# Float32-to-bf16 copies on GpSimd instead of VectorE in a fused attention and SSM kernel, with the schedule replanned

## The chip, the cores and the metric

The kernel runs on one core of a Trainium2 chip. The metric is device time in microseconds for one launch. The core has TensorE (PE, matrix products; PEld is its weight load), VectorE (DVE), ScalarE (ACT), GpSimd (POOL) and SyncE (SP), which issues nearly all DMAs here. Each engine takes its instructions in the order in which the program gives them.

## The reference

What is computed from x (2048 rows of 512) is a mix of two branches, `g * a + (1 - g) * b`:

```python
g = sigmoid((x * gate_w).sum(-1, keepdims=True))
# a: attention, 32 heads of 16, all 2048 x 2048 scores, no mask
p = softmax(einsum("bhqd,bhkd->bhqk", q, k) * 16 ** -0.5)
a = einsum("bhqk,bhkd->bhqd", p, v) @ wo        # heads joined
# b: a long convolution of each of the 512 channels, in float32 by FFT
P = exp(dt * A * l)                             # 512 x 128 complex, l = 0..2047
K = einsum("dn,dnl,dn->dl", C, P, dt * B).real
b = conv(x, K)[:2048] + x * Dskip
```

## The kernel before, in words

**Attention.** For every block b (one head pair's rows of 512 queries; 32 blocks) there are 16 key quads (kt 0 to 15) of four score tiles of 128 x 512, 2048 tiles in all. Three tiles make a group; there are 683 groups, numbered g or x. `qk(g)` computes a group's scores into one of two PSUM buffers (SC), `ex(g)` has ACT take the exponentials (ET, EX), and `pvq` multiplies them into the block's sums (OA).

**Sets.** ACT does not take all exponentials. `decide` may start a set: three key quads, whose twelve tiles are laid out over four groups so that the third tile of each group goes to DVE. There `bits` turns it into 16-bit patterns that read as bf16 exponentials (DZ), and `batch` adds three constants to all four tiles of the set with 64-bit integer adds on POOL (DU); `sums` multiplies DZ and the three DU into OA, an average of four approximations. Whether a set may start is said by this line, where `win(x)` asks for four groups since the last start and for fewer sets than `due(x)`, which runs linearly between the points of PACE:

```python
if kt < DVK - 1 and win(x) is not None and idle() >= plan["used"] \
        and (kt < DVL or not sets or f"dvp{len(sets) - 1}" in sch.flag):
```

DVK and DVL are 14; the flag `dvp{i}` is set when set i's last product has been planned. ACT's instruction has two tiles in a group with a DVE tile, and three otherwise.

**The convolution kernel K.** From parameters on DVE (`params`, `params2`) powers of the decay are built by squaring and product. `digit` writes them out as bf16 pairs (DT), `powers` and `weights` build tables for each of four quarters qr of the channels (B16, Z), with `low` and `cast` turning float32 results into bf16. `zpart` extends Z, `tables` multiplies B16 with DT (T), and `kstage(blk)` has PE multiply T with Z, transposes the result on DVE (Kt) and copies it to Ks, from where SP stores it (kd) for the convolution.

**The convolution.** `yloads` loads x (U) and K (H, in a ring of buffers that grows at the load given in HS) and `ystage` multiplies them on PE; DVE applies the gate (Yst), SP stores and reloads it (Yl). `outs` and the tail multiply the attention result with wo and add both.

**The order of work.** A planner in the kernel (`Prog`, `Sched`) runs while the program is built. Each piece of work is a segment of a thread with an engine, a cost and a priority; for every group, `fill` places the segments whose planned time comes before ACT's. The planned order is the program's order on each engine. Ops marked `lk` (float32 or bf16 work on DVE whose inputs are all in SBUF, and POOL's adds) are kept apart in the plan: a POOL op that would meet such a DVE op gets a wait for it. FILL and LOW say how much work PE should have for each group (before and after group ZEND = 260); what lacks is filled with idle products of zeros (wm).

Of the kernel before, what the change touches and what calls it, by code (L numbers as in the profile page):

```python
# [39 lines left out]
FILL = 1500  # L40
LOW = 1300
SURP = 256
FILL2 = 1500
OVER = 0.5
REST = (14, 0, 1792, 425)
# [18 lines left out]
WIN = ((0, 560, 2, 4), (560, 679, 4, 6))  # L64
PACE = ((0, 0), (40, 0), (90, 0), (140, 0), (200, 15.0), (270, 28.3), (340, 39.5), (420, 53.9), (500, 73.9), (570, 90.7), (630, 105.7), (683, 118.95))
DVEND = 679
YLP = 4.5
YQ = 0
XGO = 'g14'
YGO = 'projs'  # L70
YLGO = 'K15'
BG0 = 'g0'
BG1 = 'g0'
BG2 = 'K4'
BG3 = 'g0'
TP = 2
KP = 0.4
NB = 2
# [5 lines left out]
US = [2, 12, 3]  # L84
HS = [4, 48, 8]
BACK = 0.4
# [16 lines left out]
SPILL = 3  # L103
DVCAP = 6
DVK = 14
JS = ((2, 0, 3, 1), (1, 0, 2, 3), (0, 2, 1, 3))
DVL = 14
VW = 136
VG = 4 * VW + 16
# [629 lines left out]
def record(nc, p, B, ins):  # L739
# [138 lines left out]
    todo = []  # L878
    plan = dict(q=0, at=0, used=0.0, prev=None, wait=None, x=0)

# [9 lines left out]
    def decide(g):  # L890
        while len(tiles) < min(3 * g + 3, NSL):
            q, x = plan["q"], len(tiles) // 3
            kt = q % 16
            if kt == 0:
                plan["wait"] = None
            plan["used"] = max(plan["used"], idle() - DVCAP)
            if kt < DVK - 1 and win(x) is not None and idle() >= plan["used"] \
                    and (kt < DVL or not sets or f"dvp{len(sets) - 1}" in sch.flag):
                w = win(x)
                plan["x"] = x  # L900
                c = q if kt else q + 1
                a, b = [y for y in range(q, q + 3) if y != c]
                own, late = [4 * a + k for k in range(4)] + [4 * b + k for k in range(4)], [4 * c + k for k in JS[len(tiles) % 3]]
                js = JS[len(tiles) % 3]
                k = 0
                for _ in range(12):
                    if len(tiles) % 3 == 2:
# [12 lines left out]
                for k, x in enumerate(us):  # L920
                    held_u[x] = (len(sets) - 1, k)
                qs, plan["q"] = [a, b], q + 3
            else:
                tiles.extend(range(4 * q, 4 * q + 4))
                qs, plan["q"] = [q], q + 1
            for y in qs:
                if y < NQ - 1:
                    todo.append((y, plan["prev"], plan["wait"]))
# [211 lines left out]
    def square(o, x, conj=False):  # L1140
# [8 lines left out]
        tt("DVE", half(o, 0), half(t1, 0), half(t1, 1), ALU.subtract, [(t1, 0)], [(o, 0)], F5)  # L1149

    def digit(n):

        m, x = DIGITS.index(n), B[n]
        for qr in range(4):
            d = B[f"DT{qr}"]
            yield ("DVE", .45)
            op("DVE", lambda v, d=d, qr=qr: v.tensor_copy(d(6 * P * m, [[2 * P, 2], [2, P], [1, 2]]), x(P * qr, [[D, 2], [1, P], [0, 2]])), [(x, 0)], [(d, (m, 0))], c=.07 + .28)
            op("DVE", lambda v, d=d, qr=qr: v.tensor_scalar(d(6 * P * m + 4 * P, [[2, P], [1, 2]]), x(D + P * qr, [[1, P], [0, 2]]), -1.0, None, ALU.mult), [(x, 0)], [(d, (m, 1))], c=.07 + .14)
        sch.mark("D" + n)
# [31 lines left out]
    def params2():  # L1191
# [20 lines left out]
        yield from digit("L64")  # L1212
        yield from cmul("L80", "L64", "L16")
# [3 lines left out]
        yield from short("M9", "")  # L1217
        yield from digit("L80")

# [3 lines left out]
    def ftk(i, h):  # L1223
        return [(FT[i], x) for x in HF[h]]
# [16 lines left out]
    def weights(qr):  # L1241
# [7 lines left out]
        def cast(part, l):  # L1249
            yield ("DVE", .3)  # L1250
            op("DVE", lambda v: v.tensor_copy(Z(part * l8 + 128 * l, [[1, 256]]), FP(part * e8 + 128 * l, [[1, 256]])), rw(l, l + 1), top, c=.21)

# [26 lines left out]

    def powers(qr, last, top):  # L1280

# [36 lines left out]
        def low(part, h):  # L1318
            yield ("DVE", .55)
            op("DVE", lambda v: v.tensor_copy(place(part, h, 4), FP(part * e8 + 128 * h, [[256, 4], [32, 4], [1, 32]])),  # L1320
               rw(*range(h, 8, 2)), [top[part]], c=.42)

# [11 lines left out]
        yield from cross(3, lambda part: FP(part * e8 + 768, one), rw(6), one)  # L1334
        yield ("DVE", .4)
        op("DVE", lambda v: v.memset(FP(0, one), 1.0), [], rw(0), c=.1)
        op("DVE", lambda v: v.memset(FP(e8, one), 0.0), [], rw(0), c=.1)
        op("DVE", lambda v: v.tensor_copy(last(256, [[l8, 2], [512, 4], [2, 32]]), fp(qr, ZT["L8"], [[PS, 2], [32, 4], [1, 32]])), fk(qr, ZT["L8"]), lo, c=.34)
# [14 lines left out]
    def zpart(qr):  # L1353
# [8 lines left out]
        def mul(u, i):  # L1362
            k, dn, at, part = units[u]
            Dm, xr, yr = B[dn], i, part if i == 0 else 1 - part
            yield ("DVE", H10)
            tt("DVE", lambda: FT[i].b16(1024 * (u % 2), [[128, 8], [1, 128]]), lambda: Z(xr * 4096, [[128, 8], [1, 128]]),
               lambda: Dm(yr * D + 128 * qr, [[0, 8], [1, 128]]), ALU.mult,
               [(Z, 3, qr), (Z, 5, qr), (Dm, (0, 0))] + ([(Dm, (0, 1))] if dn == "DL32" else []), ftk(i, u % 2), H10)

# [19 lines left out]
    def park():  # L1389
# [7 lines left out]
        sch.mark("pd")  # L1397

    def ploads():
        yield ("AFTER", "pd")  # L1400
        for qr, go in enumerate((BG0, BG1, BG2, BG3)):
            Z = B[f"Z{qr % NZ}"]
            yield ("AFTER", go)
            if qr >= NZ:
                yield ("AFTER", f"KT{4 * (qr - NZ) + 3}")
            for k0, n, over, at in ((0, 2, [3, 5], 256), (2, 2, [(1, 0), (1, 1)], 640), (4, 1, [(0, 0), (0, 1)], 1024), (5, 3, [(2, 0), (2, 1)], 1536)):
# [7 lines left out]
    def bases():  # L1414
        for qr, go in enumerate((BG0, BG1, BG2, BG3)):
            yield ("AFTER", go)
            B16 = B[f"B16{qr % NB}"]
            if qr >= NB:
                yield ("AFTER", f"T{4 * (qr - NB) + 3}")
            yield from powers(qr, B16, [(B16, 0), (B16, 2)])  # L1420
            yield from weights(qr)
# [4 lines left out]
    def tables():  # L1426
        for qr in range(4):
# [3 lines left out]
            for blk in range(4 * qr, 4 * qr + 4):  # L1431
                Tm, c0 = B[f"T{tbuf(blk)}"], CB * (blk % 4)
                bk = [(B16, 0), (B16, 2), (B16, (1, 0)), (B16, (1, 4))]
                old = [k for k in range(blk) if tbuf(k) == tbuf(blk)]
# [22 lines left out]
    def kstage(blk):  # L1457
        qr = blk // 4
        Z, Ks = B[f"Z{qr % NZ}"], B[f"Ks{blk % 2}"]
        zk = [(Z, 3, qr), (Z, 5, qr)] + [(Z, (k, p_), qr) for k in range(3) for p_ in range(2)]  # L1460
        Tm = B[f"T{tbuf(blk)}"]
# [4 lines left out]
        for k in range(8):  # L1466
# [20 lines left out]
        sch.unlock("MB")  # L1487
        yield ("DVE", .6)
        op("DVE", lambda v: v.tensor_copy(Ks(HW, [[5 * HW, 2], [8, 4], [HW // 2, 8], [1, 8]]), Kt(0, [[256, 2], [64, 4], [8, 8], [1, 8]])),
           [(Kt, 0, blk), (Ks, "z")], [(Ks, (0, q), blk) for q in range(2)], c=.36)  # L1490
        for q in range(2):
            op("DVE", lambda v, q=q: v.tensor_copy(Ks(q * HW // 2 + 1 - q, [[5 * HW, 2], [8, 4], [1, 7 + q]]), Kt(48 + 7 * q, [[256, 2], [64, 4], [1, 7 + q]])),
               [(Kt, 0, blk), (Ks, "z")], [(Ks, (1, q), blk)], c=.13)
        sch.mark(f"K{blk}")
# [532 lines left out]
```

## Time and profile before

| | us |
|---|---|
| median of three runs | 752.06 |
| the three runs | 754.86, 752.06, 751.84 |
| span of the profiled execution, first to last instruction | 750.5 |
| busy: PE / DVE / ACT / POOL | 685.3 / 657.1 / 732.4 / 362.2 |
| mean granted TensorE clock | 0.997 |

The span is that of one execution, and its own whole time is not recorded beside it; the median of the runs lies 1.6 us above it. A stretch's busy time compared with its length says which engine is full there; an engine's idle time matters only where another engine, in the end ACT, waits for it. In a row of groups the columns are line, engine, operation, written and read tiles with shapes, count, busy us and mean ns of one, then the idle time ahead and what ended it. Most instructions are recorded by a helper, so one source line (L754 for products, L1111 for DVE's two-input work) stands for many places, and the tile names tell them apart.

### The profile page before, as it was taken

The page shows a single profiled execution, that of the slowest core. Times are in us where ns is not written, and L with a number is a line of the kernel's source. Part 1 is how long each engine was busy: PE and PEld are TensorE (multiplying, and loading weights), DVE is VectorE, ACT ScalarE, POOL GpSimd, SP SyncE. Part 2 cuts the span into 40 slices and gives each one's busy share as a digit, 9 for nine tenths or more (in the row PEclk, how much of TensorE's full clock was granted, in tenths as well). Part 3 has the DMA queues.
Part 4 walks back from the last instruction along what each step waited for, and adds up shares of the span by engine and source line. Part 5 has one row for each costly group of instructions (what it writes and reads, how often), then busy time and mean ns, then how long its engine had stood idle before and what let it go on. Part 6 is the DMA issues. An engine that isn't in the chain of part 4 may idle for free.

```text
span 750.5 us, 31408 instructions
## 1 busy us (share of the span) xinstructions
PE 685.3 (91%) x13915; PEld 289.6 (39%) x13916; DVE 657.1 (88%) x1105; ACT 732.4 (98%) x696; POOL 362.2 (48%) x362
## 2 busy tenths in 40 slices
PE   8777877888999999999999999999999999999997
PEld 4222332443434444434545344544443442222222
DVE  7999999999888888989989789999887878787876
ACT  7999999999999999999999999999999999999996
POOL 3000000000157777564453654577778777777673
PEclk9999999999999999999999999999999999999999
DMA  9767810312566447767369787727576675000000
GB/s 218 164 150 143 169 45 7 67 45 68 119 164 163 122 127 181 196 158 189 62 160 224 182 230 207 183 57 187 137 185 146 145 175 115 26 19 27 19 16 29
DMA packets 176588, 94.33 MB, mean 126 GB/s; under 512 B 116802, under 2 KB 159940, under 8 KB 176452
## 3 DMA queue, kind: packets, MB, share of 16 engines
q1 hardware_dynamic: 175492, 91.48, 51.1%
q8 instruction: 109, 1.79, 1.0%
q10 hardware_dynamic: 960, 0.85, 0.4%
q14 instruction: 27, 0.22, 0.1%
HBM read 63.42 MB, written 18.90 MB: 110 GB/s over the span
## 4 chain that ended last, share of the span: by engine, by line
ACT 77%; PE 16%; DVE 3%; DMA 1%; POOL 1%; issue 1%; SPq 0%; DVEq 0%; POOLq 0%
ACT ET L1017 63%; ACT EX L1017 14%; PE SC L754 6%; PE OA L754 6%; PE MB L754 3%; DMA H<-gm_kd 1%; DVE DZ L1039 1%; POOL DU L1058 1%; DVE ft L1111 1%; DVE T L1111 0%; DVE OT L1079 0%; SPq L1408 0%; DVE Yst L1592 0%; DVE OnT L1103 0%; DVE Qm L1886 0%
## 5 line engine op out<-in xcount | busy, mean ns | idle before, releaser
L1017 ACT ACTIVATE ET<-SC 128x1024 bf16<-128x1024 f32 (+1 forms) x537 | 592.2, 1357 | 6.4 <-PE SC L754 4.9
L1058 POOL INT64_ADD DU<-DZ x342 | 354.7, 1051 | 374.2 <-DVE DZ L1039 257.1
L1039 DVE TENSOR_SCALAR DZ<-SC 128x512 uint16<-128x512 f32 x460 | 308.2, 685 | 63.2 <-PE SC L754 53.0
L754 PE MATMUL SC<-Qm,KT 32*128 32x512 bf16 x2048 | 274.2, 385 | 49.2 <-ACT ET L1017 41.7
L754 PEld LDWEIGHTS SC<-Qm,KT 32*128 32x128 bf16 x2048 | 70.0, 91 | 252.8 <-ACT ET L1017 168.1
L1017 ACT ACTIVATE EX<-SC 128x1024 bf16<-128x1024 f32 (+1 forms) x146 | 149.8, 1238 | 1.5 <-PE SC L754 1.4
L754 PE MATMUL OA<-DU,VE 128*32 128x512 bf16 x1380 | 132.6, 385 | 2.7 <-POOL DU L1058 2.7
L754 PE MATMUL OA<-ET,VE 128*32 128x512 bf16 x1281 | 132.3, 388 | 0.4 <-ACT ET L1017 0.2
L754 PEld LDWEIGHTS MB<-U,H 128*32 128x32 bf16 x4096 | 84.0, 144 | 30.8 <-issue 20.9
L754 PE MATMUL MB<-U,H 128*32 128x128 bf16 (+7 forms) x4096 | 92.6, 225 | 3.0 <-issue 1.5
L754 PE MATMUL OA<-wm 128*32 128x256 bf16 (+3 forms) x317 | 60.1, 344 | 1.2 <-DVE idf L809 1.2
L1111 DVE TENSOR_TENSOR T<-B,DT 128x1536 bf16<-128x1536 bf16 x64 | 60.8, 978 | 0.1
L754 PEld LDWEIGHTS OA<-DU,VE 128*32 128x32 bf16 x1380 | 36.4, 97 | 47.2 <-issue 34.0
L754 PEld LDWEIGHTS OA<-ET,VE 128*32 128x32 bf16 x1281 | 33.8, 95 | 50.0 <-issue 47.2
L754 PEld LDWEIGHTS MB<-T,Z 128*32 128x32 bf16 x2048 | 43.8, 155 | 10.9 <-issue 7.3
L754 PE MATMUL MB<-T,Z 128*32 128x64 bf16 (+1 forms) x2048 | 47.1, 235 | 0.0
L754 PE MATMUL OA<-DZ,VE 128*32 128x512 bf16 x460 | 45.7, 385 | 0.0
L1111 DVE TENSOR_TENSOR ft<-Z 128x512 f32<-128x512 f32 (+3 forms) x48 | 39.9, 856 | 0.8 <-DMA Z<-gm_pd 0.7
L754 PE MATMUL OA<-EX,VE 128*32 128x512 bf16 x307 | 38.6, 385 | 0.0
L1111 DVE TENSOR_TENSOR Z<-ft,ft 128x1024 bf16<-128x1024 bf16 (+3 forms) x56 | 32.3, 576 | 0.5
L1592 DVE TENSOR_TENSOR Yst<-MB,gt 128x512 bf16<-128x512 f32 x32 | 21.9, 685 | 6.2 <-PE MB L754 6.0
L1079 DVE STREAM_TRANSPOSE OT<-OA 128x512 f32<-128x512 f32 x32 | 22.8, 714 | 2.2 <-PE OA L754 1.8
(143 smaller groups left out, 415.4 us busy)
## 6 DMA issues: line engine op xcount, KB each, us to landing
H<-gm_kd SPq DMA_DIRECT2D x128, 256.0 KB, 4.3
U<-gm_xs SPq DMA_DIRECT2D x128, 134.2 KB, 3.9
T<-B SPq DMA_DIRECT2D x16, 256.0 KB, 2.6
gm_yd<-Yst SPq DMA_DIRECT2D x64, 64.0 KB, 3.3
gm_kd<-Ks SPq DMA_DIRECT2D x64, 40.0 KB, 1.8
gm_xs<-xP SPq DMA_DIRECT2D x16, 136.0 KB, 5.0
gm_pd<-L SPq DMA_DIRECT2D x8, 256.0 KB, 4.1
Z<-gm_pd SPq DMA_DIRECT2D x8, 256.0 KB, 3.8
```

Source lines behind the costliest of these rows:

```text
L754: op("PE", lambda t: t.matmul(out(), lhsT(), rhs(), start=start, stop=stop, skip_group_check=True, **kw), R, W, c=c, lat=.15, a=a, cfg=cfg)
L1017: op("ACT", lambda a: a.activation(E(at, [[1, 512 * n]]), sc(0, [[1, 512 * n]]), AF.Exp, scale=DH ** -0.5), [(sc, i, g) for i in range(n)] ...
L1039: op("DVE", lambda v: v.tensor_scalar(z.u16(512 * k, [[1, 512]]), sc(1024, [[1, 512]]), XS, XB, ALU.mult, ALU.add), [(sc, 2, g)], [(z, k, ...
L1058: op("POOL", lambda v, u=u, cut=cut: v.int64_add(u.u64(), z.u64(), cut * 0x0001000100010001), R, [(u, 0, i)], c=1.016, lat=.09, lk=True)
L1079: op("DVE", lambda v: v.transpose(OT(512 * w, [[1, 512]]), OA(0, [[1, 512]])), [(OA, 0, b)], [(OT, w, b)], c=.64)
L1111: op(eng, lambda v: v.tensor_tensor(o(), a(), b_(), f), R, W, c=c)
L1592: op("DVE", lambda v, w=w, h=h: v.tensor_tensor(Yst(1024 * w + 4 * h, [[128, R8], [8, 16], [1, 4]]), MB(0, [[1, R8], [R8, 16], [NC, 4]]), ...
```

## The change

104 copies of DVE go to POOL: 24 in `digit`, 16 `cast` in `weights`, 16 `low` in `powers`, and 48 from Kt to Ks in `kstage`, as do eight memsets in `powers`. They become POOL segments (`GP` = -1 is their priority) with a planned cost of 0.15 us + 1 ns an element, and are marked `lk`. `digit` runs in threads of its own. Slices of the tiles get finer names, so that readers wait for the copies they need. Sets may also start on key quads 13 to 15 in groups 490 to 659, and a set that runs into the next block is told to both blocks. Constants of the plan differ. What is left out here are renamed slices only.

```diff
-LOW = 1300
+LOW = 1250
-OVER = 0.5
+OVER = 0.48
-PACE = ((0, 0), (40, 0), (90, 0), (140, 0), (200, 15.0), (270, 28.3), (340, 39.5), (420, 53.9), (500, 73.9), (570, 90.7), (630, 105.7), (683, 118.95))
+PACE = ((0, 0), (40, 0), (65, 0.1), (90, 0.1), (140, 0.18), (200, 15.36), (267, 27.79), (340, 38.94), (420, 53.39), (500, 73.48), (570, 92.46), (630, 110.41), (683, 124.32))
-YLP = 4.5
+YLP = 4.15
-XGO = 'g14'
+XGO = 'g24'
-YLGO = 'K15'
+YLGO = 'K14'
-BG2 = 'K4'
-BG3 = 'g0'
+BG2 = 'K5'
+BG3 = 'K3'
-KP = 0.4
+KP = 0.17
-HS = [4, 48, 8]
+HS = [4, 56, 8]
-DVCAP = 6
+DVCAP = 6.38
+STRX = 490
+STRE = 660
+STRK = (13, 14, 15)
+GF = .15
+GP = -1
+GE = .001
...
-            if kt < DVK - 1 and win(x) is not None and idle() >= plan["used"] \
+            if q + 2 < NQ and (kt < DVK - 1 or STRX <= x < STRE and kt in STRK) and win(x) is not None and idle() >= plan["used"] \
                     and (kt < DVL or not sets or f"dvp{len(sets) - 1}" in sch.flag):
                 w = win(x)
                 plan["x"] = x
-                c = q if kt else q + 1
+                c = next(y for y in range(q, q + 3) if 0 < y % 16 < 15)
...
-                plan["wait"] = f"dvp{len(sets)}"
+                plan["wait"][c // 16] = f"dvp{len(sets)}"
...
+    def gc(n):
+        return GF + n * GE
+
+    def gop(fn, R, W, n):
+        op("POOL", fn, R, W, c=gc(n), lat=.09, lk=True)
...
-            yield ("DVE", .45)
-            op("DVE", lambda v, d=d, qr=qr: v.tensor_copy(d(6 * P * m, ...), x(P * qr, ...)), ...)
-            op("DVE", lambda v, d=d, qr=qr: v.tensor_scalar(d(6 * P * m + 4 * P, ...), x(D + P * qr, ...), -1.0, None, ALU.mult), ...)
+            yield ("POOL", gc(512), GP)
+            gop(lambda v, d=d, qr=qr: v.tensor_copy(...), [(x, 0)], [(d, (m, 0))], 512)
+            yield ("POOL", gc(256), GP)
+            gop(lambda v, d=d, qr=qr: v.tensor_scalar(...), [(x, 0)], [(d, (m, 1))], 256)
...
-        yield from digit("L16")
+        sch.add(digit("L16"), 2)
...
         def cast(part, l):
-            yield ("DVE", .3)
-            op("DVE", lambda v: v.tensor_copy(...), rw(l, l + 1), top, c=.21)
+            yield ("POOL", gc(256), GP)
+            gop(lambda v: v.tensor_copy(...), rw(l, l + 1), [(Z, ("c", part, l), qr)], 256)
...
         def low(part, h):
-            yield ("DVE", .55)
-            op("DVE", lambda v: v.tensor_copy(place(part, h, 4), ...), rw(*range(h, 8, 2)), [top[part]], c=.42)
+            yield ("POOL", gc(512), GP)
+            gop(lambda v: v.tensor_copy(place(part, h, 4), ...), rw(*range(h, 8, 2)), [(last, ("t", part, h))], 512)
...
-        yield ("DVE", .4)
-        op("DVE", lambda v: v.memset(FP(0, one), 1.0), [], rw(0), c=.1)
-        op("DVE", lambda v: v.memset(FP(e8, one), 0.0), [], rw(0), c=.1)
+        yield ("POOL", .4)
+        op("POOL", lambda v: v.memset(FP(0, one), 1.0), [], fk(qr, ("f", 0)), c=.2)
+        op("POOL", lambda v: v.memset(FP(e8, one), 0.0), [], fk(qr, ("f", 0)), c=.2)
...
-        yield ("DVE", .6)
-        op("DVE", lambda v: v.tensor_copy(Ks(HW, ...), Kt(0, ...)), ..., c=.36)
+        yield ("POOL", gc(512) + 2 * gc(64), GP)
+        gop(lambda v: v.tensor_copy(Ks(HW, ...), Kt(0, ...)), ..., 512)
         for q in range(2):
-            op("DVE", lambda v, q=q: v.tensor_copy(Ks(...), Kt(...)), ..., c=.13)
+            gop(lambda v, q=q: v.tensor_copy(Ks(...), Kt(...)), ..., 64)
```

More of the change, by code (lines that the diff above doesn't have):

```diff
@@ L878, in record @@
     todo = []
-    plan = dict(q=0, at=0, used=0.0, prev=None, wait=None, x=0)
+    plan = dict(q=0, at=0, used=0.0, prev=None, wait={}, x=0)
     def idle():
@@ L893, in decide @@
             kt = q % 16
-            if kt == 0:
-                plan["wait"] = None
             plan["used"] = max(plan["used"], idle() - DVCAP)
-            if kt < DVK - 1 and win(x) is not None and idle() >= plan["used"] \
+            if q + 2 < NQ and (kt < DVK - 1 or STRX <= x < STRE and kt in STRK) and win(x) is not None and idle() >= plan["used"] \
                     and (kt < DVL or not sets or f"dvp{len(sets) - 1}" in sch.flag):
@@ L927, in decide @@
                 if y < NQ - 1:
-                    todo.append((y, plan["prev"], plan["wait"]))
+                    todo.append((y, plan["prev"], plan["wait"].get(y // 16)))
                 plan["prev"] = y
@@ L1155, in digit @@
             d = B[f"DT{qr}"]
-            yield ("DVE", .45)
-            op("DVE", lambda v, d=d, qr=qr: v.tensor_copy(d(6 * P * m, [[2 * P, 2], [2, P], [1, 2]]), x(P * qr, [[D, 2], [1, P], [0, 2]])), [(x, 0)], [(d, (m, 0))], c=.07 + .28)
-            op("DVE", lambda v, d=d, qr=qr: v.tensor_scalar(d(6 * P * m + 4 * P, [[2, P], [1, 2]]), x(D + P * qr, [[1, P], [0, 2]]), -1.0, None, ALU.mult), [(x, 0)], [(d, (m, 1))], c=.07 + .14)
+            yield ("POOL", gc(512), GP)
+            gop(lambda v, d=d, qr=qr: v.tensor_copy(d(6 * P * m, [[2 * P, 2], [2, P], [1, 2]]), x(P * qr, [[D, 2], [1, P], [0, 2]])), [(x, 0)], [(d, (m, 0))], 512)
+            yield ("POOL", gc(256), GP)
+            gop(lambda v, d=d, qr=qr: v.tensor_scalar(d(6 * P * m + 4 * P, [[2, P], [1, 2]]), x(D + P * qr, [[1, P], [0, 2]]), -1.0, None, ALU.mult), [(x, 0)], [(d, (m, 1))], 256)
         sch.mark("D" + n)
@@ L1211, in params2 @@
         sch.mark("WN")
-        yield from digit("L64")
+        sch.add(digit("L64"), 2)
         yield from cmul("L80", "L64", "L16")
@@ L1217, in params2 @@
         yield from short("M9", "")
-        yield from digit("L80")
+        sch.add(digit("L80"), 2)
     FT = [B["ft1"], B["ft2"]]
@@ L1249, in cast @@
         def cast(part, l):
-            yield ("DVE", .3)
-            op("DVE", lambda v: v.tensor_copy(Z(part * l8 + 128 * l, [[1, 256]]), FP(part * e8 + 128 * l, [[1, 256]])), rw(l, l + 1), top, c=.21)
+            yield ("POOL", gc(256), GP)
+            gop(lambda v: v.tensor_copy(Z(part * l8 + 128 * l, [[1, 256]]), FP(part * e8 + 128 * l, [[1, 256]])), rw(l, l + 1), [(Z, ("c", part, l), qr)], 256)
         def mul(i, m, ln):
@@ L1278, in weights, with powers @@
         sch.unlock("FT")
-    def powers(qr, last, top):
+    def powers(qr, last):
         e8, l8 = PS, last.free // 2
@@ L1318, in low @@
         def low(part, h):
-            yield ("DVE", .55)
-            op("DVE", lambda v: v.tensor_copy(place(part, h, 4), FP(part * e8 + 128 * h, [[256, 4], [32, 4], [1, 32]])),
-               rw(*range(h, 8, 2)), [top[part]], c=.42)
+            yield ("POOL", gc(512), GP)
+            gop(lambda v: v.tensor_copy(place(part, h, 4), FP(part * e8 + 128 * h, [[256, 4], [32, 4], [1, 32]])),
+                rw(*range(h, 8, 2)), [(last, ("t", part, h))], 512)
         yield ("LOCK", "FT")
@@ L1334, in powers @@
         yield from cross(3, lambda part: FP(part * e8 + 768, one), rw(6), one)
-        yield ("DVE", .4)
-        op("DVE", lambda v: v.memset(FP(0, one), 1.0), [], rw(0), c=.1)
-        op("DVE", lambda v: v.memset(FP(e8, one), 0.0), [], rw(0), c=.1)
+        yield ("POOL", .4)
+        op("POOL", lambda v: v.memset(FP(0, one), 1.0), [], fk(qr, ("f", 0)), c=.2)
+        op("POOL", lambda v: v.memset(FP(e8, one), 0.0), [], fk(qr, ("f", 0)), c=.2)
+        yield ("DVE", .34)
         op("DVE", lambda v: v.tensor_copy(last(256, [[l8, 2], [512, 4], [2, 32]]), fp(qr, ZT["L8"], [[PS, 2], [32, 4], [1, 32]])), fk(qr, ZT["L8"]), lo, c=.34)
@@ L1367, in mul @@
                lambda: Dm(yr * D + 128 * qr, [[0, 8], [1, 128]]), ALU.mult,
-               [(Z, 3, qr), (Z, 5, qr), (Dm, (0, 0))] + ([(Dm, (0, 1))] if dn == "DL32" else []), ftk(i, u % 2), H10)
+               fk(qr, *ZTOP) + [(Dm, (0, 0))] + ([(Dm, (0, 1))] if dn == "DL32" else []), ftk(i, u % 2), H10)
         def add(u):
@@ L1397, in park @@
         sch.mark("pd")
+    ZTOP = [3, 5] + [("c", part, l) for part in range(2) for l in (0, 2)]
     def ploads():
@@ L1405, in ploads @@
                 yield ("AFTER", f"KT{4 * (qr - NZ) + 3}")
-            for k0, n, over, at in ((0, 2, [3, 5], 256), (2, 2, [(1, 0), (1, 1)], 640), (4, 1, [(0, 0), (0, 1)], 1024), (5, 3, [(2, 0), (2, 1)], 1536)):
+            for k0, n, over, at in ((0, 2, ZTOP, 256), (2, 2, [(1, 0), (1, 1)], 640), (4, 1, [(0, 0), (0, 1)], 1024), (5, 3, [(2, 0), (2, 1)], 1536)):
                 yield ("SP", .6)
@@ L1419, in bases @@
                 yield ("AFTER", f"T{4 * (qr - NB) + 3}")
-            yield from powers(qr, B16, [(B16, 0), (B16, 2)])
+            yield from powers(qr, B16)
             yield from weights(qr)
@@ L1432, in tables @@
                 Tm, c0 = B[f"T{tbuf(blk)}"], CB * (blk % 4)
-                bk = [(B16, 0), (B16, 2), (B16, (1, 0)), (B16, (1, 4))]
+                bk = [(B16, ("t", part, h)) for part in range(2) for h in range(2)] + [(B16, (1, 0)), (B16, (1, 4))]
                 old = [k for k in range(blk) if tbuf(k) == tbuf(blk)]
@@ L1459, in kstage @@
         Z, Ks = B[f"Z{qr % NZ}"], B[f"Ks{blk % 2}"]
-        zk = [(Z, 3, qr), (Z, 5, qr)] + [(Z, (k, p_), qr) for k in range(3) for p_ in range(2)]
+        zk = fk(qr, *ZTOP) + [(Z, (k, p_), qr) for k in range(3) for p_ in range(2)]
         Tm = B[f"T{tbuf(blk)}"]
@@ L1487, in kstage @@
         sch.unlock("MB")
-        yield ("DVE", .6)
-        op("DVE", lambda v: v.tensor_copy(Ks(HW, [[5 * HW, 2], [8, 4], [HW // 2, 8], [1, 8]]), Kt(0, [[256, 2], [64, 4], [8, 8], [1, 8]])),
-           [(Kt, 0, blk), (Ks, "z")], [(Ks, (0, q), blk) for q in range(2)], c=.36)
+        yield ("POOL", gc(512) + 2 * gc(64), GP)
+        gop(lambda v: v.tensor_copy(Ks(HW, [[5 * HW, 2], [8, 4], [HW // 2, 8], [1, 8]]), Kt(0, [[256, 2], [64, 4], [8, 8], [1, 8]])),
+            [(Kt, 0, blk), (Ks, "z")], [(Ks, (0, q), blk) for q in range(2)], 512)
         for q in range(2):
-            op("DVE", lambda v, q=q: v.tensor_copy(Ks(q * HW // 2 + 1 - q, [[5 * HW, 2], [8, 4], [1, 7 + q]]), Kt(48 + 7 * q, [[256, 2], [64, 4], [1, 7 + q]])),
-               [(Kt, 0, blk), (Ks, "z")], [(Ks, (1, q), blk)], c=.13)
+            gop(lambda v, q=q: v.tensor_copy(Ks(q * HW // 2 + 1 - q, [[5 * HW, 2], [8, 4], [1, 7 + q]]), Kt(48 + 7 * q, [[256, 2], [64, 4], [1, 7 + q]])),
+                [(Kt, 0, blk), (Ks, "z")], [(Ks, (1, q), blk)], 64)
         sch.mark(f"K{blk}")
```

## The prediction

> **What bounds the kernel now.** I read the busy line of the page first, then the table of 50 us stretches, then what ScalarE (ACT) waited for. Columns of the stretches: start and end, length, busy time of PE, PEld, DVE, ACT and POOL with instruction counts, granted clock, DMA share, GB/s.
>
> ```profile
> PE 685.3 (91%) x13915; PEld 289.6 (39%) x13916; DVE 657.1 (88%) x1105; ACT 732.4 (98%) x696; POOL 362.2 (48%) x362
> ```
>
> ```profile
> 100.00:150.00 50.00, 40.63 (x940) 17.32 (x936) 48.76 (x86) 50.00 (x38) 0.00 (x0) 1.00 0.17 42
> ...
> 200.00:250.00 50.00, 47.41 (x1001) 20.97 (x997) 44.63 (x80) 48.12 (x50) 31.38 (x30) 1.00 0.52 133
> 250.00:300.00 50.00, 48.09 (x1043) 21.95 (x1035) 43.50 (x72) 48.48 (x52) 36.43 (x35) 1.00 0.60 154
> ...
> 400.00:450.00 50.00, 45.47 (x1074) 22.07 (x1064) 42.98 (x69) 48.21 (x48) 25.80 (x24) 1.00 0.87 214
> 450.00:500.00 50.00, 47.05 (x1165) 23.71 (x1161) 45.37 (x73) 48.99 (x49) 27.21 (x27) 1.00 0.66 167
> 500.00:550.00 50.00, 49.39 (x1062) 23.02 (x1054) 46.08 (x76) 49.23 (x53) 36.34 (x36) 1.00 0.58 141
> ...
> 650.00:700.00 50.00, 49.21 (x582) 12.29 (x583) 40.09 (x63) 50.00 (x54) 39.58 (x40) 1.00 0.07 21
> ```
>
> ACT's exponentials are the bound: 98% of the span, and all of the 50 us in stretches such as 100 to 150 and 650 to 700 us. In the middle it loses 1.88 + 1.52 + 1.79 + 1.01 + 0.77 = 7.0 us. VectorE (DVE) is nearly as full, but ACT does not wait for it directly:
>
> ```profile
> ACT ET L1017 <- PE SC L754: 4.9, 12, 1.0
> ```
>
> ACT's lost time is TensorE (PE) being late with scores (SC). Why PE is late shows in the chain of waits around one such stall (start, length, what):
>
> ```profile
> 239.33 1.29 DVE DZ L1039 x2
> 240.62 1.14 DVE ft L1111
> 241.76 0.09 issue
> 241.84 1.05 POOL DU L1058
> 242.89 0.04 issue
> 242.94 0.40 PE OA L754 x3
> 243.34 0.33 PE SC L754 x4
> ```
>
> Two conversions (DZ) and a product (ft) on DVE come before an integer add on GpSimd (POOL, DU); PE takes its instructions in order, so the sums (OA) that need the add hold up the scores behind them.
>
> **What a set is worth.** A "set" takes four score tiles from ACT: four groups of exponentials have two tiles instead of three, and the third goes to DVE (DZ, the "bits") and then to three adds on POOL. All bits, and those of one full stretch (there the third number after the length is DVE, the fourth POOL):
>
> ```profile
> L1039 DVE TENSOR_SCALAR DZ<-SC 128x512 uint16<-128x512 f32 x460 | 308.2, 685 | 63.2 <-PE SC L754 53.0 <-POOL DU L1058 5.6 <-PE OA L754 0.5
> ```
>
> ```profile
> 650.00:700.00 50.00, 5.10 (x52) 1.35 (x52) 33.79 (x51) 39.58 (x40) 1.00 0.07 21
> ```
>
> Without sets ACT does 38 groups in 50 us (100 to 150), 1.316 us each. From 650 to 700 us it does 54, of which 51 gave a tile away: (50 - 3 x 1.316) / 51 = 0.903 us. A tile is worth 0.413 us, a set 1.65 us.
>
> **The change, part by part.** *The number of sets* follows from the planner's rule. A set may start when fewer have started than PACE allows, four groups after the last one, on key quad 0 to 12 of a block of 16 quads (21.33 groups). Counted with the old PACE this gives 115, and the trace has 460 = 4 x 115 bits, so the rule is all that limits them. From group 490 on the limit is not PACE but the block's end: starts at quads 0, 3, 6, 9 and 12. The change lets quads 13, 14 and 15 start a set there and raises PACE to 124.32. But the clause with DVL = 14 stays: at quad 14 or 15 the last products of the set before must have been planned. After a start at quad 12 the next decision falls at quad 15, four groups on, when that set's fourth bits have not even been issued. So quad 15 stays plain, and the next set starts at quad 0 as now; from 0 in steps of three, quad 13 is never met. I count 45 sets from group 490 on, as before, and ahead of it 69 instead of 70, since PACE is lower between groups 270 and 500 (53.39 for 53.9 at 420); one of them now sits at group 42, where PACE is no longer zero. Total 114: one set fewer, **+1.65 us** of ACT. If I misread the clause, the same count without it gives 116.
>
> *The copies.* What leaves DVE, and the nearest POOL rows (busy us, mean ns):
>
> ```profile
> L1320 DVE CAST B<-Z 128x512 bf16<-128x512 f32 x16 | 8.7, 545 | 0.0
> L1489 DVE CAST Ks<-Kt 128x512 bf16<-128x512 f32 x16 | 7.4, 463 | 0.2
> L1157 DVE CAST DT<-L 128x512 bf16<-128x512 f32 x12 | 5.0, 420 | 0.0
> L1251 DVE CAST Z<-Z 128x256 bf16<-128x256 f32 x16 | 4.9, 309 | 0.0
> L1158 DVE TENSOR_SCALAR DT<-L 128x256 bf16<-128x256 f32 x12 | 3.4, 287 | 0.0
> L1492 DVE CAST Ks<-Kt 128x64 bf16<-128x64 f32 x16 | 3.0, 188 | 0.0
> L1492 DVE CAST Ks<-Kt 128x56 bf16<-128x56 f32 x16 | 3.0, 186 | 0.0
> L1336 DVE MEMSET Z<- 128x128 f32 x4 | 0.7, 165 | 0.0
> L1058 POOL INT64_ADD DU<-DZ x342 | 354.7, 1051 | 374.2 <-DVE DZ L1039 257.1 <-DVE ft L1111 46.7 <-DVE T L1111 26.0
> L1510 POOL MEMSET xP<- 128x256 bf16 x4 | 1.1, 339 | 0.0
> L780 POOL MEMSET Dr<- 128x512 bf16 x1 | 0.5, 520 | 0.0
> L1639 POOL MEMSET gt<- 128x128 f32 x1 | 0.2, 245 | 0.0
> L782 POOL MEMSET sel<- 128x32 bf16 x1 | 0.1, 133 | 0.0
> ```
>
> DVE is rid of 8.7 + 7.4 + 5.0 + 4.9 + 3.4 + 3.0 + 3.0 us and of eight memsets of 0.165 us: 36.7 us. No POOL copy is in this trace. One of 512 elements lies between the memset of 512 (0.52 us, which only writes) and the add of 512 eight-byte words (1.05); one of 256 between 0.34 and half an add, 0.53; the small ones between 0.13 and 0.25. The change's planner books 0.15 us + 1 ns an element: 0.66, 0.41, 0.21. [...] POOL gains 44 x 0.66 + 28 x 0.41 + 32 x 0.21 + 8 x 0.245 = 49 us (39 to 71 by the bounds) and loses three adds, 3.2 us: 362 becomes 408. This costs the span nothing by itself, since POOL idles 374 us. If that cover is gone, the adds behind a copy leave later, and PE waits at the sums.
>
> What now waits: a Ks copy stands behind up to a batch of adds, 3.2 us, and behind it wait the next K stage, the kd stores on SP and the H loads after them. The 16 copies spread over 435 us (rows below), 29 us apart on average, which covers it. The digit copies fall where POOL has nothing else to do; behind them wait the first tables.
>
> *What the freed DVE time buys.* Not sets (above). It can only win back ACT's 7.0 us. In the stall shown DVE and POOL hold 1.29 + 1.14 + 1.05 us of the chain; in others PE's own products do. Bounds: 0, if waits on POOL eat it, and 7.0. I take the middle, **-3.5 us**.
>
> *Beside each other.* The same copy takes different times on DVE (ns min/median/max, first to last start in us):
>
> ```profile
> L1320 DVE CAST B<-Z x16: 434/468/1287, 89.0 to 420.1; 128x512 bf16<-128x512 f32 x16
> L1489 DVE CAST Ks<-Kt x16: 406/418/757, 136.6 to 571.3; 128x512 bf16<-128x512 f32 x16
> ```
>
> The longest is 0.85 us over the shortest, less than one add. So I take it that copy and add exclude each other, while bits and adds do not (33.79 + 39.58 us in 50). On POOL the copies would hold up DVE's products in the same way: 37 us of exclusive time become 49, 12 us more. I cost that at nothing because the bits run meanwhile; without that cover it is rival C. [...]
>
> *The small edits.* LOW 1250 asks for fewer idle products (wm) after group 260, and the H ring grows at load 56 instead of 48:
>
> ```profile
> 350.00:400.00 50.00, 0.40 (x4) 0.10 (x4) 0.00 (x0) 1.00 0.54 131
> ```
>
> ```profile
> PE OA L754 <- POOL DU L1058: 2.7, 5, 1.0
> ...
> PE MB L754 <- DMA H<-gm_kd: 1.5, 3, 0.9
> ```
>
> Idle products are 0.40 us of PE there, and the clock is granted at 1.00: nothing. Eight more H loads use the small ring: between 0 and 8 x 0.9 = 7 us; I take 0, as PE waited only three times for H in all. XGO moves the x transposes 10 groups, 13 us, back on SP's queue, into the stretch where the DMA share sinks to 0.17: nothing. BG2, BG3 and YLGO shift loads by about a K stage on that queue, past Qm and H loads; between 650 and 700 us the DMA share is 0.07, so there is room behind them: nothing. Of OVER, DVCAP, KP and YLP no row shows an effect.
>
> *The sum.* 750.5 + 1.65 - 3.5 = 748.6 us of span. The profile states only the span; the median of the runs, 752.06, lies 1.6 above it: **750.2 us**. That is within half a per cent, 3.8 us, about what this kernel's runs can tell from no change.
>
> **The rivals.**
> A, *no relief*: PE's own load makes the stalls, and the freed time lies idle: 752.06 + 1.65 = 753.7. For it: PE is busy 47.4 and 48.1 of 50 us where ACT loses most. Against: the chain above.
> B, *faster*: the stalls all go, 752.06 + 1.65 - 7.0 = 746.7; and if sets do cross block ends (116 of them, -1.65 instead of +1.65), 743.4. For it: 36.7 us of DVE is much beside 7.0. Against: POOL's new work queues with the adds. That the crossing does not happen is part of my forecast; here it does.
> C, *slower: adds late behind copies*. At the upper bounds 71 - 49 = 22 us of POOL are unplanned; by the copies' times (89 to 571 us) about half of it, 11 us, falls where sets run. If half of this reaches ACT through the sums and nothing is won back: 752.06 + 1.65 + 5.5 = 759.2. It decides from 2.1 us of new stalls on (755.8). For it: POOL is busy 31 to 40 of 50 us where sets are dense, and PE did wait 2.7 us for adds. Against: POOL idled 257 us waiting for bits alone. [...]
>
> **How the numbers follow.** My forecast has 0.40 (747.5 to 752.9, a quarter of it under 748.3), A 0.18, B 0.22, C 0.20. Faster by over 0.5%: 0.10 + 0.22 = 0.32. Slower: C, and 0.02 of A's upper end: 0.22. Within: 0.46. The range leaves out a tenth on each side: the lower half of B (under 744.8) and the upper half of C (over 758).
>
> **What would show it.** Right: 456 bits; 128x512 casts on POOL near 0.66 us; ACT losing about 3.5 us between 200 and 550 us; PE waiting for DU no longer than now. Wrong: 464 bits or more (the clause lets sets through); casts near 1 us with PE waiting longer for DU (C); ACT still losing 7 us (A).

## The result and the profile after

The changed kernel takes 770.72 us (median of 4 runs, 770.14 to 771.37) against 753.46 us of the kernel before (4 runs, 751.84 to 756.28) measured beside it: ratio 1.024, interval 1.021 to 1.0269. It is slower by 17 us; the forecast was 750.2 and its range ended at 758. (One of the 21 executions of the kernel before that stand beside e5 to e8 below took 881.8 us at a granted clock of 0.573; medians and ratios leave it out.) Here are the busy line, two of the 50 us stretches (columns as before) and the whole middle as one stretch.

```profile
PE 691.9 (90%) x13927; PEld 290.0 (38%) x13927; DVE 634.7 (83%) x989; ACT 734.7 (96%) x696; POOL 421.3 (55%) x471
```

```profile
50.00:100.00 50.00, 34.30 (x688) 12.56 (x676) 35.25 (x59) 41.84 (x34) 19.00 (x26) 0.91 0.64 134
100.00:150.00 50.00, 37.19 (x854) 16.02 (x854) 38.77 (x58) 41.81 (x31) 7.53 (x11) 0.89 0.22 48
```

```profile
200.00:650.00 450.00, 426.98 (x9501) 197.71 (x9497) 379.06 (x579) 443.55 (x438) 290.16 (x312) 1.00 0.63 159
```

The span grew by 768.3 - 750.5 = 17.8 us, ACT's work by only 734.7 - 732.4 = 2.3. The other 15.5 us are idle time of ACT, and they lie in one place: from 50 to 150 us ACT loses 8.16 + 8.19 = 16.4 us, where it lost 0.2 before. The long stretch from 200 to 650 us, where the relief was to come, loses 6.5 us; the kernel before lost 7.3 us there. Two rows of the kernel before:

```profile
50.00:100.00 50.00, 40.06 (x892) 16.24 (x892) 47.64 (x98) 49.84 (x39) 0.00 (x0) 0.97 0.76 153
...
200.00:650.00 450.00, 428.95 (x9346) 196.23 (x9338) 391.14 (x635) 442.75 (x446) 285.48 (x275) 1.00 0.64 155
```

The waits of ACT, PE and POOL (total us, times, longest) name one chain.

```profile
ACT ET L1021 <- PE SC L760: 18.3, 12, 8.5
PE OA L760 <- POOL DU L1062: 17.2, 7, 9.1
POOL DU L1062 <- issue: 13.3, 2, 7.4
```

ACT waits for scores, PE for integer adds, and POOL twice for nothing that the wait's row shows. The timelines of POOL, of PE (only the products that read DU) and of ACT show where (start, length, what, idle before and its releaser):

```profile
49.13 1.12 POOL L1169 TENSOR_SCALAR DT<-L 128x256 bf16<-128x256 f32 x1 [7.04 <-issue]
...
71.35 0.85 POOL L1169 TENSOR_SCALAR DT<-L 128x256 bf16<-128x256 f32 x1
78.15 2.05 POOL L1062 INT64_ADD DU<-DZ  x2 [5.95 <-issue]
83.83 0.61 POOL L1167 CAST DT<-L 128x512 bf16<-128x512 f32 x1 [3.63 <-DVE DM L1177]
91.53 0.90 POOL L1169 TENSOR_SCALAR DT<-L 128x256 bf16<-128x256 f32 x1 [7.08 <-DVE ft L1115]
...
95.87 0.85 POOL L1169 TENSOR_SCALAR DT<-L 128x256 bf16<-128x256 f32 x1
104.10 1.03 POOL L1062 INT64_ADD DU<-DZ  x1 [7.39 <-issue]
```

```profile
79.24 0.62 PE L760 MATMUL OA<-DU,VE 128*32 128x512 bf16 x4 [6.06 <-POOL DU L1062]
105.19 0.62 PE L760 MATMUL OA<-DU,VE 128*32 128x512 bf16 x4 [9.10 <-POOL DU L1062]
```

```profile
81.30 2.79 ACT L1021 ACTIVATE ET<-SC 128x1536 bf16<-128x1536 f32 x2 [5.88 <-PE SC L760]
106.82 1.45 ACT L1021 ACTIVATE ET<-SC 128x1536 bf16<-128x1536 f32 x1 [8.49 <-PE SC L760]
```

This is the one set that the change moved to group 42. Its three adds stand in POOL's queue among the digit negations of L1169, and each change between the two kinds of instruction is followed by 6 to 7 us in which POOL does nothing. The views of the two source lines show a further instruction that the timeline leaves out:

```profile
L1169 POOLq MODIFY_POOL_CONFIG  x4: 11/12/12, 42.1 to 84.5; - x4
L1062 POOLq MODIFY_POOL_CONFIG  x4: 12/13/14, 72.4 to 96.9; - x4
```

Before the first negation, before the first add, and again for each after the alternation, a pair of these rows stands in POOL's queue: at 42.1, 72.4, 84.5 and 96.9 us. From each pair to the first instruction of the new kind it takes 49.13 - 42.1 = 7.0, 78.15 - 72.4 = 5.8, 91.53 - 84.5 = 7.0 and 104.10 - 96.9 = 7.2 us. What the trace shows is the rows and a gap of 5.8 to 7.2 us after them, at every alternation. That the gap is a load of code, as the expectations below call it, was my reading of the row's name; no run shows what POOL does in it.

ACT's waits behind the two late adds are 5.88 + 8.49 = 14.4 of its 16.4 us. Not all of this is the gap right ahead of the add. The negation at 91.53 us waited for DVE's product ft as well, which ended at 91.03, and the add at 104.10 for DVE's product B, which came late because it stood behind these negations. The chain of waits ends with B and then 4.0 us of idle time with no further release in the profile, by theory 1 below part of the gap:

```profile
99.50 0.59 DVE B L1115
100.09 4.01 issue
```

What these changes of kind cost together is read from e1 below.

### The profile page after: what moved, and what is told of

The parts are those of the page before. It is cut to its first block, busy times and chain, and to the rows that moved or that the text cites. A ratio compares the mean times of both kernels' runs of the same rounds, so it can differ in the third digit from the quotient of the medians.

```text
span 768.3 us, 31471 instructions
## 1 busy us (share of the span) xinstructions
PE 691.9 (90%) x13927; PEld 290.0 (38%) x13927; DVE 634.7 (83%) x989; ACT 734.7 (96%) x696; POOL 421.3 (55%) x471
## 4 chain that ended last, share of the span: by engine, by line
ACT 75%; PE 14%; DVE 4%; issue 2%; POOL 2%; DMA 1%; SPq 1%; DVEq 0%; POOLq 0%
ACT ET L1021 59%; ACT EX L1021 16%; PE SC L760 6%; PE OA L760 6%; PE MB L760 3%; DVE DZ L1043 2%; POOL DU L1062 1%; DMA H<-gm_kd 1%; DVE ft L1115 1%; SPq L1618 0%; POOL DT L1169 0%; DVE OT L1083 0%; POOL DT L1167 0%; DVE ON L1100 0%; SPq L1562 0%
## 5 line engine op out<-in xcount | busy, mean ns | idle before, releaser
L1062 POOL INT64_ADD DU<-DZ x339 | 349.0, 1046 | 162.9 <-DVE DZ L1043 66.2
L760 PE MATMUL OA<-wm 128*32 128x256 bf16 (+3 forms) x344 | 63.7, 347 | 1.2 <-DVE idf L815 1.2
L1503 POOL CAST Ks<-Kt 128x512 bf16<-128x512 f32 x16 | 9.9, 617 | 80.2 <-DVE T L1115 74.6
L1115 DVE TENSOR_TENSOR ft<-Z 128x512 f32<-128x512 f32 (+3 forms) x48 | 41.6, 886 | 0.6
```

What stands on the lines that cost most here:

```text
L760: op("PE", lambda t: t.matmul(out(), lhsT(), rhs(), start=start, stop=stop, skip_group_check=True, **kw), R, W, c=c, lat=.15, a=a, cfg=cfg)
L1062: op("POOL", lambda v, u=u, cut=cut: v.int64_add(u.u64(), z.u64(), cut * 0x0001000100010001), R, [(u, 0, i)], c=1.016, lat=.09, lk=True)
L1115: op(eng, lambda v: v.tensor_tensor(o(), a(), b_(), f), R, W, c=c)
L1503: gop(lambda v: v.tensor_copy(Ks(HW, [[5 * HW, 2], [8, 4], [HW // 2, 8], [1, 8]]), Kt(0, [[256, 2], [64, 4], [8, 8], [1, 8]])), [(Kt, 0, b ...
```

## The experiments

Theory 1 is this gap at each change of kind (the "load" of the expectations): the sums of the early set wait for its adds, the adds for the gap, and PE takes instructions in order (before its sums at 105.19 us it stood 9.10 us, and ACT stood 8.49 us until the scores behind them were there). Theory 2 is rival C of the prediction: POOL's copies are slower than planned and hold the adds up. All ratios are against the kernel before on the same chip; its median in the three batches was 752.32 (e1 to e4b), 753.73 (e5 to e8) and 752.58 us (e9, e10). A ratio is an estimate over all runs of both kernels, so it can differ a little from the quotient of two medians. Runs of different batches are best compared by their ratios.

| run | median us | ratio, interval |
|---|---|---|
| e1: negations become copies | 754.25 | 1.0015, 0.9995 to 1.0035 |
| e2: e1 and one early scratch add | 754.3 | 1.0023, 0.9999 to 1.0046 |
| e3: before, one negation at group 600 | 762.91 | 1.0139, 1.0109 to 1.0169 |
| e4b: e2 with sets across block ends | 755.31 | 1.0023, 1.0 to 1.0047 |
| e5: all copies on POOL, old plan | 765.17 | 1.015, 1.0111 to 1.0188 |
| e6: casts on POOL, negations on DVE, old plan | 753.14 | 0.9987, 0.9966 to 1.0007 |
| e7: before, one negation at group 30 | 753.14 | 0.9993, 0.9964 to 1.0021 |
| e8: replan alone | 758.29 | 1.0061, 1.0031 to 1.0091 |
| e9: e5 and one scratch add at group 75 | 757.59 | 1.0064, 1.0037 to 1.009 |
| e10: e6 with sets across block ends | 760.66 | 1.0109, 1.0058 to 1.016 |

**e1, no change of kind.** The twelve negations stay on POOL as copies, which leaves out the sign of a third of DT.

```diff
-gop(lambda v, d=d, qr=qr: v.tensor_scalar(d(...), x(...), -1.0, None, ALU.mult), ..., 256)
+gop(lambda v, d=d, qr=qr: v.tensor_copy(d(...), x(...)), ..., 256)
```

> The changed kernel with its twelve negations on POOL turned into plain copies of the same shape (the sign of a third of DT is left out); the plan is the same. Theory 1, code loads: each change of POOL between the negation (TENSOR_SCALAR) and the 64-bit add costs a load of about 6 to 7 us, four in all, and two of them stop PE and ACT at the early set (5.9 and 8.5 us). Without the negation only the first load, before the first add, is left: ACT's lost time from 50 to 150 us falls from 16.4 to 6 or 7 us, and the time from 770.7 to 761 to 763. Theory 2, late copies: the adds of the early set stand in POOL's queue behind digit copies that wait for DVE, whatever the kind of copy: ACT still loses 15 us or more there, 768 to 772.

754.25 us: 16.5 us come back (15.3 when each is taken against the kernel before beside it), and ACT loses 0.8 us from 50 to 150 us instead of 16.4 (the two stretches). All other 92 copies are still on POOL, in the same plan.

```profile
50.00:100.00 50.00, 39.29 (x903) 16.11 (x903) 43.18 (x67) 49.57 (x41) 19.25 (x31) 1.00 0.69 141
100.00:150.00 50.00, 41.74 (x1048) 19.40 (x1048) 47.23 (x74) 49.64 (x38) 8.64 (x13) 1.00 0.34 70
```

Theory 2 falls: the copies that remain cost almost nothing. But I had expected one gap of 6 us before the first add to stay, and it did not. The source line and POOL's timeline say why:

```profile
L1062 POOLq MODIFY_POOL_CONFIG  x2: 11/11/11, 71.5 to 71.5; - x2
```

```profile
72.36 1.04 POOL L1062 INT64_ADD DU<-DZ  x1 [0.90 <-DVE DZ L1043]
```

The pair of rows stands there at 71.5 us, and the add starts 0.9 us later, released by its bits. So the rows alone are no proof of a gap of 6 us: ahead of the adds' first use there is none of this size, only at a change to the negation (7.0 us in the changed kernel) or from it back to the adds (5.8 and 7.2 us). e1 also makes each of the twelve shorter (0.40 us instead of 0.85), 5.4 us of POOL in all, so it does not show the gaps alone; e3, e7 and e9 do.

**e2, the same with an add of eight words ahead.** In group 3, on a scratch tile:

```diff
+if g == 3:
+    op("POOL", lambda v: v.memset(B["scr"](0, [[1, 16]]), 0.0), ...)
+    op("POOL", lambda v: v.int64_add(B["scr"].u64(), B["scr"].u64(), 1), ...)
```

> [...] Theory 1: no load is left near the early set, ACT loses under 1 us from 50 to 150 us, and the time is 753 to 757 (753.5 of the kernel before, one set fewer +1.65, slow copies on POOL 0 to 2). Theory 2: 768 to 772 as before.

754.3 us, equal to e1: there was no gap left to take away. The scratch add itself waited for none; its rows stand at 14.3 us:

```profile
14.47 0.19 POOL L1936 INT64_ADD scr<-scr  x1
```

**e3 and e7, the gap by itself.** The kernel before, with nothing moved, gets one negation of 8 elements on POOL: in group 600 amid the sets (e3) or in group 30, long before the first (e7). A memset of the scratch tile goes ahead of it, in group 100 or 20 (not shown in the diff below).

```diff
+if g == 600:      # e7: g == 30
+    op("POOL", lambda v: v.tensor_scalar(B["scr"](8, [[1, 8]]), B["scr"](0, [[1, 8]]), -1.0, None, ALU.mult), ...)
```

> The kernel before with one negation of eight elements on POOL in group 600, among the adds. Theory 1: two loads of 6 to 7 us delay the next batch of adds by 12 to 15 us, PE waits for them in order, and after what the queue's idle time takes up the time rises by 8 to 13 us, to 761 to 766. Theory 2: eight elements are 0.1 us, the time stays within 1 us of 753.5.

> The kernel before with one 8-element negation on POOL in group 30, long before the first add. Theory 1: the load goes into POOL's idle time; ACT loses nothing that it did not lose before, and the time is that of the kernel before within 0.5% (750 to 756 us). Rival (a TENSOR_SCALAR on POOL costs some 10 us wherever it stands): 761 to 766 us, as with the same instruction in group 600.

Both as theory 1 says. In e3 an instruction of 0.27 us costs 10.6 us. POOL's timeline and ACT's:

```profile
667.53 0.27 POOL L1923 TENSOR_SCALAR scr<-scr 128x8 bf16<-128x8 bf16 x1 [6.87 <-issue]
673.54 6.17 POOL L1059 INT64_ADD DU<-DZ  x6 [5.74 <-issue]
```

```profile
675.82 1.02 ACT L1018 ACTIVATE ET<-SC 128x1024 bf16<-128x1024 f32 x1 [9.94 <-PE SC L755]
```

POOL stands 6.87 + 5.74 = 12.6 us, ACT 9.9 of them. In e7 the same instruction has its gap at 15 us (from 15.3 to 22.7 us, 7.4 us), and the rows of the way back stand at 24.3 us, long before the first add at 204 us, which waits for its bits and not for a gap; the time is that of the kernel before. From the source lines:

```profile
L1923 POOLq MODIFY_POOL_CONFIG  x2: 11/11/11, 15.3 to 15.3; - x2
L1923 POOL TENSOR_SCALAR scr<-scr x1: 1206/1206/1206, 22.7 to 22.7; 128x8 bf16<-128x8 bf16 x1
L1059 POOLq MODIFY_POOL_CONFIG  x2: 6/6/6, 24.3 to 24.3; - x2
```

**e5 and e9, all copies without the early set.** The changed kernel with PACE and the other planning constants of before (PACE is 0 until group 140 again); e9 adds the scratch add of e2 in group 75, after the last negation.

```diff
-PACE = ((0, 0), (40, 0), (65, 0.1), (90, 0.1), (140, 0.18), ...)
+PACE = ((0, 0), (40, 0), (90, 0), (140, 0), ...)
```

> The changed kernel, with all its copies, negations and memsets on POOL, but PACE and the eleven other planning constants as before the change: 115 sets, and none before group 140. Theory 1 (code loads between negations and adds, paid by ACT only where adds stand among the negations): the negations are all done before the first add, the load falls in idle time, ACT loses under 1 us from 50 to 150 us, and the time is 752 to 756 us. Rival (twelve negations on POOL, each behind slow copies, delay the tables and with them the sets): ACT still loses several us after 100 us and the time is above 758 us.

> The kernel of the run with all copies on POOL and the old plan, which lost 4.3 us of ACT at 212 us, where POOL's first add had waited 5.85 us for nothing that the profile shows, right behind a Ks copy that itself came late. New here: an add of eight words of a scratch tile in group 75 (about 115 us), after the last negation and before the first set. Theory 1 (the load runs where the instruction stands in POOL's queue, and costs what is queued behind it): the scratch add waits some 6 us for nothing shown while POOL is idle, the first real add follows its bits at once, ACT loses 3 to 6 us from 200 to 300 us instead of 11.4, and the time is 754 to 759 us. Rival (that run's slowness comes from the plan with copies on POOL, whatever the load does): 763 to 767 us.

e5 was a miss: I had put the one gap left into idle time, and the kernel takes 765.17 us. ACT loses only 0.6 us from 50 to 150 us, but 11.4 from 200 to 300, where the kernel before lost 3.4. The negations end at 100 us, yet the rows of the way back stand at 208.5 us, behind a Ks copy that itself waited for DVE, and the add starts 5.6 us after them (the row of L1503, then the first add; then ACT):

```profile
206.91 0.61 POOL L1503 CAST Ks<-Kt 128x512 bf16<-128x512 f32 x1 [7.44 <-DVE Kt L1500]
207.47 0.80 POOL L1506 CAST Ks<-Kt 128x56 bf16<-128x56 f32 x2
214.12 2.05 POOL L1062 INT64_ADD DU<-DZ  x2 [5.85 <-issue]
```

```profile
216.93 1.03 ACT L1021 ACTIVATE ET<-SC 128x1024 bf16<-128x1024 f32 x1 [4.28 <-PE SC L760]
```

The gap did not fall into idle time: POOL idled about 90 of the 108 us between the last negation and these rows, and that did not help, as the rows stood in the wrong place of the queue. e9 puts them into the right one, and the time falls by 7.6 us (6.4 when each is taken against the kernel before beside it), within theory 1's forecast:

```profile
L1936 POOLq MODIFY_POOL_CONFIG  x2: 11/11/11, 105.1 to 105.2; - x2
L1936 POOL INT64_ADD scr<-scr x1: 2726/2726/2726, 110.8 to 110.8; - x1
```

```profile
205.78 1.04 POOL L1063 INT64_ADD DU<-DZ  x1
```

The gap now runs from 105.1 to 110.8 us and the real adds follow their copy at once. ACT still loses 6.1 us from 200 to 300 us, just over the 3 to 6 that I had given: 5.3 of e5's 11.4 us went with the gap, and 2.7 us more than in the kernel before stay unexplained. e6, which has KP 0.17 instead of 0.4 and the negations on DVE, loses only 3.5 us there, so one of these two is the place to look; no run parts them.

**e6 and e8, the move and the replan apart.** e6 has the 92 casts and the memsets on POOL, the negations on DVE, and the constants of before except KP. e8 is the reverse: every copy on DVE, and all new constants except PACE.

> As the kernel before in its planning constants except KP .17 (how far ahead of its use a K stage is spread); the 92 casts and eight memsets on POOL, the twelve negations on DVE. 115 sets, no TENSOR_SCALAR on POOL. If the DVE time set free buys ACT time (the prediction's relief of 3.5 us), ACT loses about 3.5 us from 200 to 650 us and the time is 748 to 750 us; if it buys nothing (theory 2: PE's own load and the chain over the adds hold the scores), ACT loses 6 to 8 us there and the time is 752 to 755 us. I expect the second.

> The kernel before, every copy on DVE, with the changed planning constants except PACE (LOW, OVER, YLP, XGO, YLGO, BG2, BG3, KP, HS, DVCAP): 115 sets. The prediction put these edits at nothing: 750 to 756 us, and ACT loses about 7 us from 200 to 650 us as in the kernel before. If one of them hurts by itself (H ring grown later, x transposes ten groups later, K stages spread otherwise): more than 757 us, with a longer wait of PE for H or for K.

The middle of e6 and that of e8, as one stretch each:

```profile
200.00:650.00 450.00, 429.29 (x9275) 194.44 (x9275) 377.09 (x582) 443.29 (x446) 303.58 (x324) 1.00 0.64 155
```

```profile
200.00:650.00 450.00, 429.91 (x9216) 193.18 (x9213) 387.61 (x631) 439.69 (x441) 280.98 (x271) 0.99 0.63 155
```

In e6 ACT loses 450 - 443.29 = 6.7 us, against 7.3 before: a lighter DVE (377 instead of 391 us busy) buys 0.6 us in these two traces, and the time is that of the kernel before. In e8 ACT loses 10.3 us, and the time is 758.29, above the 757 at which I had called one of the edits harmful. Which edit does it is open; PE waits for H in no row of e8's list of waits, and ACT's wait for the last output is 5.8 us instead of 3.2. e2 and e8 share those constants (e2 has the new PACE besides), and by the ratios e2 is about 0.4%, 3 us, faster: under the new constants the casts on POOL seem to win back much of what the constants cost. That compares two batches, and no run shows it by itself.

**e4b and e10, sets across block ends.** The clause that kept quads 14 and 15 plain is lifted, in e2 (116 sets) and in e6 (117 sets).

```diff
-DVL = 14
+DVL = 16
```

> As e2_copy_preload, with DVL 16 instead of 14, so that the quads 14 and 15 may start a set and sets do cross block ends: 116 sets instead of 114 by the counting rule (464 bits instead of 456). If a set is worth 1.65 us of ACT, 3.3 us less than e2_copy_preload. Rival: the sums of a crossing set come late to the norm at the block end and PE waits there, so nothing is won or up to 5 us lost.

> The run with the casts on POOL, the negations on DVE and the old plan, with the clause for quads 14 and 15 lifted (DVL 16): 117 sets instead of 115, so ACT has 3.3 us less to do. If ACT's work is the bound after 490 us, where it is busy all of each 50 us, the time falls by 2 to 3.5 us to 749.5 to 751.5 us, which would be the best version; if the tail (MB products, output) takes it back, as in the earlier crossing run, 752 to 755 us. I give the second 60%.

ACT's work falls to 730.9 and 728.9 us (by 3.3 and 3.4 for two sets, as the forecast's 1.65 a set would have it), and neither run is faster. e4b ends as its rival had it, though late sums at a block's end were not shown to be the reason; e10's 760.66 us lies above both ranges that I had given, a miss. In e4b ACT loses 2.66 + 2.40 us from 250 to 350 us (1.28 + 0.50 in e2). In both, the wait of the last output grows (it was 3.5 us in e2); the rows are of e6, e4b and e10:

```profile
ACT fo L2003 <- PE MB L760: 4.1, 1, 4.1
```

```profile
ACT fo L2007 <- PE MB L761: 7.2, 1, 7.2
```

```profile
ACT fo L2003 <- remote: 13.8, 1, 13.8
```

After e10's last exponentials the chain of waits runs through output work left over, products and DVE's additions in turn, four times, 2.2 us each (the first here):

```profile
739.09 0.93 ACT EX L1021
...
740.47 1.11 PE MB L760 x20
...
741.66 0.70 DVE fo L1734
```

In e6 the same four additions start between 713.8 and 739.9 us, beside the exponentials; in e10 between 741.7 and 748.3, behind them. So in e10 output work lies uncovered behind a shorter ACT; why the planner placed it there is open. No version beat the kernel before by more than these runs can tell.

## Why the prediction was wrong

*The step that failed* is "This costs the span nothing by itself, since POOL idles 374 us", with its companion, "The digit copies fall where POOL has nothing else to do". In its paragraph on the sets the prediction had found the early set ("one of them now sits at group 42, where PACE is no longer zero") and priced it as a set, not as three adds amid the digits. What stands between those adds and the negations, the pairs of rows with a gap after each, had no price at all. The measured price is a gap of 5.8 to 7.2 us on POOL at each change, four of them, two ahead of adds that PE waits for: 14.4 us of ACT stand in the waits behind these adds, and e1, without the changes, is 15.3 us faster. The trace of before held a hint, in the view of the adds' source line:

```profile
L1058 POOLq MODIFY_POOL_CONFIG  x2: 51/51/51, 10.1 to 10.1; - x2
```

The prediction took no account of rows of POOL's queue that are not work, and so did not ask when such a row comes again. By itself the row could not have given the price: before the adds' first use at most 0.9 us (e1) and 0.1 us (e2) lie behind it.

*The sign of the rivals.* C had the right path (adds late, PE in order, ACT short of scores) and the wrong cause. Its price of 5.5 us came from copies at their upper bounds; in sum the copies did nearly reach these (66 us below, for 69 by the bounds), and cost nothing measurable (e6).

*Copies on POOL*, rows of the changed kernel (busy us, mean ns):

```profile
L1331 POOL CAST B<-Z 128x512 bf16<-128x512 f32 x16 | 15.2, 974 | 15.0 <-DVE ft L1115 9.3 <-DVE B L1115 5.2 <-PE MB L760 0.5
L1506 POOL CAST Ks<-Kt 128x56 bf16<-128x56 f32 (+1 forms) x32 | 12.6, 425 | 0.0
L1169 POOL TENSOR_SCALAR DT<-L 128x256 bf16<-128x256 f32 x12 | 11.0, 918 | 18.8 <-DVE ft L1115 7.1 <-issue 7.0 <-DVE pt L1115 4.1
L1503 POOL CAST Ks<-Kt 128x512 bf16<-128x512 f32 x16 | 9.9, 617 | 80.2 <-DVE T L1115 74.6 <-DVE B L1322 3.4 <-DVE ft L1115 1.2
L1262 POOL CAST Z<-Z 128x256 bf16<-128x256 f32 x16 | 9.4, 592 | 14.5 <-DVE ft L1115 8.5 <-DVE Z L1115 5.2 <-DVE ON L1100 0.8
L1167 POOL CAST DT<-L 128x512 bf16<-128x512 f32 x12 | 7.8, 654 | 16.7 <-DVE M L1150 6.7 <-DVE pt L1115 4.1 <-DVE DM L1177 3.6
```

Together 66 us, where the step had 47 of its 49 for them: 0.66 was right for two kinds of 512 elements (0.617 and 0.654), low for the third (0.974), and the 0.41 and 0.21 were low for the casts of 256 (0.592) and half the true value for the negation (0.918) and the small copies (0.425); all three passed even the upper bounds of 0.53 and 0.25. The size was off, the conclusion for the casts was not.

*Sets.* 456 bits were counted in the trace, 114 sets, as read from the clause; +1.65 us of ACT was forecast, and ACT's busy time grew by 2.3 us in the changed kernel and by 1.8 in e2 (734.2 for 732.4). Right, as far as such a sum can tell: in e8, with the old number of sets, it is 733.2.

*The relief* of 3.5 us, the middle between two bounds, was 0.6 us in e6 and 0.8 in the changed kernel (0.8 in e2, 1.8 in e1). Rival A had this: PE is as busy as before in those stretches (426.98 for 428.95 of 450 us). That PE's own load and not DVE made the other stalls is A's reading; no run here changed PE's load. Without the gaps and without relief the forecast's terms give A's 753.7; e1 measured 754.25. That they meet so closely is partly luck, since the constants alone cost 0.6% (e8), which A does not have.

*Small edits at nothing*: together they cost about 0.6% by themselves (e8), which the forecast had at 0.

## What to carry to other kernels

Before moving an operation to GpSimd, list the kinds of instruction that this engine will then run in turn, not only its idle time: here a change between negations and integer adds came with a gap of 5.5 to 7.7 us each time, and the gap came where the change stood in the queue (208.5 us in e5, 105.1 us in e9). Look among the rows of the engine's queue for those that are not work, here `MODIFY_POOL_CONFIG`, and ask who waits for the first instruction after each; if a change must be, put a dummy of the next kind where the engine idles and nobody waits (e9). And an engine with hundreds of idle microseconds (POOL here: 768.3 - 421.3 = 347) can still be late by seven (7.39) at the one place where PE, in order, waits for it (9.10).

## What the runs showed of the hardware

- On POOL, plain casts and memsets ran between integer adds without a `MODIFY_POOL_CONFIG` row (in the changed kernel none stands after 96.9 us, with casts and memsets among the adds from 104 us on); a TENSOR_SCALAR did not. From the row to the first instruction a change to it took 6.9 to 7.7 us (the changed kernel, e3, e5, e7, e9), a change back to the adds 5.5 to 7.2 us (the changed kernel, e3, e5, e9; 5.5 in e3 and 5.7 in e9, where the add waited for nothing else), while the first adds started at most 0.9 us (e1) and 0.1 us (e2) after their rows.
- Stretches of 50 us with a stall of PE of 6 to 10 us show a lower mean granted clock: 0.91 and 0.89 in the changed kernel from 50 to 150 us, where 0.97 and 1.00 stood before, and 0.86 in e3 from 650 to 700 us, where 1.00 stood before.
- A negation of 256 elements on POOL took 0.85 us, a cast of the same tile 0.40 us (medians 852 and 401 ns, the latter in e1).
